# V loaded by casting transfers on the software queue, and channel halves interleaved in V, u and W1

## The chip, the cores and the metric

One core of one Trainium2 chip. The metric is device time in microseconds (us), lower is better. Where two kernels are compared, the ratio is the mean time of one kernel's fast runs over that of the kernel before in the same rounds on the same chip, so not quite the ratio of the medians that are quoted beside it.

## The reference

```python
# u, v: (8, 3008, 256); z: (8, 3008, 64); w_in: (256, 2048); w_out: (2048, 256); all fp32
scores = matmul(z, z.transpose(0, 2, 1)) / 3008
attn   = maximum(scores, 0) ** 2
x      = u * matmul(attn, v)                 # per batch
h      = x.reshape(24064, 256) @ w_in
out    = (h * sigmoid(1.702 * h)) @ w_out
```

## The kernel before

For each of 8 batches the kernel makes the squared scores `a` (matmul "sc", relu on ScalarE, "ACT", square on VectorE, "DVE"), multiplies them with V into `o` (the attention phase, six query chunks), gates `o` with the transposed u into `xt`, and makes the up product `hg` and the down products `st` and `yp`. Scores are symmetric, so about half of the blocks of `a` are not computed but made by DMA transposes (`tt<-a`, `ad<-a`) that the SP engine issues. Transfers that SP issues go by a hardware queue, those that Pool (GpSimd) issues by the software queue. TensorE keeps its order and waits if such a block is late.

V is the stationary operand, in fp16, and 256 channels are two loads of 128 columns (`c` is 0 or 1). In the kernel before, fp32 V comes by the SP queue into a staging tile, and Pool casts it into `V16`, regrouping the channels into two packed halves:

```python
vst = pu.tile([P, VB, D], F32, name="vst", tag="vst", bufs=3)
eng.dma_start(vst[:, :full, :], v[b, ...])                       # SP queue, 512 KB
for k in range(NCC):                                             # 2 casts per 4 key blocks
    pool.tensor_copy(V16[b][:, n0:n0 + VB, k, :].rearrange("p n (q c) -> p n q c", c=QW),
                     vst.rearrange("p n (q k c) -> p n q k c", k=NCC, c=QW)[:, :, :, k, :])
...
# attention: two matmuls on 64 rows each run side by side (upper half of one key block, lower half)
ins = pe.matmul(acc[c][:, :n], V16[b][h, j, c, :], weights(b, i, j)[h], ...)
...
# u comes by Pool's (software) queue; four 128 KB transfers per query chunk, 256-byte runs
eng.dma_start(uq[k * QW:(k + 1) * QW, :n // QW]..., src[:, :, cs])
...
# blocks by symmetry, issued by SP
sp.dma_start_transpose(TT[b, i, cj][:, k0:k0 + 2]..., a...)
...
LOAD = {(3, NJ + 4): 4, (4, NJ + 5): 5}    # (chunk, step of attention): u chunk to load
```

Of the kernel before, what the change touches and what calls it, by code (L numbers as in the profile page):

```python
# [9 lines left out]
F32 = mybir.dt.float32  # L10
F16 = mybir.dt.float16
P = 128
# [3 lines left out]
def kernel(  # L16
# [16 lines left out]
    B, S, D = u.shape  # L33
# [3 lines left out]
    NJ = (S + P - 1) // P  # L37
    S0 = (S // P) * P
    SREM = S - S0
    CH = 512  # L40
# [3 lines left out]
    NCC = D // P  # L44
# [3 lines left out]
    QW = 32  # L48
# [7 lines left out]
    dve, act, pe, sp, pool = nc.vector, nc.scalar, nc.tensor, nc.sync, nc.gpsimd  # L56
# [98 lines left out]

    VB = 4

    def load_v(b, n0, eng):


        if n0 == 0:
            V16[b] = pz.tile([P, NJ, NCC, P], F16, name="V16", tag="V16")
        if b or n0 < 3 * VB:
            vst = pu.tile([P, VB, D], F32, name="vst", tag="vst", bufs=3)
        else:
            vst = pa.tile([P, VB, D], F32, name="vst", tag="tt", bufs=14)
        full = min(VB, NJ - 1 - n0)
        eng.dma_start(vst[:, :full, :], v[b, n0 * P:(n0 + full) * P].rearrange("(n p) c -> p n c", p=P))
        if full < VB:
            for h in range(2):  # L170
                eng.dma_start(vst[h * SREM:(h + 1) * SREM, full, :], v[b, S0:S])
        for k in range(NCC):
            pool.tensor_copy(  # L173
                V16[b][:, n0:n0 + VB, k, :].rearrange("p n (q c) -> p n q c", c=QW),
                vst.rearrange("p n (q k c) -> p n q k c", k=NCC, c=QW)[:, :, :, k, :],
            )

    def width(i):
        return CH if i < NCH - 1 else LAST
# [1 line left out]
    def load_u(b, i):  # L181
        eng = pool if b or i else sp
        n = width(i)
        uq = pu.tile([P, CH // QW, NCC, QW], F32, name="uq", tag="uq")
        src = u[b, i * CH:i * CH + n].rearrange("(q t) c -> t q c", t=QW)
        for k in range(P // QW):
            cs = slice(k * NCC * QW, (k + 1) * NCC * QW)
            eng.dma_start(uq[k * QW:(k + 1) * QW, :n // QW].rearrange("t q k c -> t q (k c)"), src[:, :, cs])  # L188
        UQ[b, i] = uq

    def turn_u(b, i):
        n = width(i)
        ut = pu.tile([P, NCC, CH // QW, QW], F32, name="ut", tag="ut")
        UT[b, i] = ut
        dve.transpose(ut[:, :, :n // QW, :].rearrange("p k q t -> p q k t"), UQ.pop((b, i))[:, :n // QW])



# [84 lines left out]
    def attend(b, i, both=False):  # L283


        n = width(i)
        js, cs = list(range(NJ - 1)), range(2)
        own = i * CB
        if b == 0 and i in (3, 4):
            js = js[own:-CB + 1] + js[:own] + js[-CB + 1:]  # L290
        elif b and i == NCH - 3:
            js = js[own:own + 2] + js[own + CB:-CB + 1] + js[:own] + js[own + 2:own + CB] + js[-CB + 1:]
        elif b and i < NCH - 2:
            js = js[own:own + 2] + js[own + CB:-CB + 1] + js[own + 2:own + CB] + js[:own] + js[-CB + 1:]
        half = [(0, TOP, NJ - 1), (1, LOW, NJ - 1)]
        if both:
            order = [[(c, FULL, j)] for j in js[:-CB] for c in cs] + [[(c, FULL, j)] for c in cs for j in js[-CB:]]
            order.insert(-CB, half)
        elif i == NCH - 1:
            order = [half] + [[(c, FULL, j)] for c in cs for j in js]  # L300
        else:
            order = [[(0, TOP, j), (1, LOW, j)] for j in js] + [half] + [[(1, TOP, j), (0, LOW, j)] for j in js]
        flat = [(k, m) for k, ms in enumerate(order) for m in ms]
        first = {c: next(m for m in flat if m[1][0] == c) for c in cs}
        final = {c: [m for m in flat if m[1][0] == c][-1] for c in cs}
        acc, turn = {}, NJ if order[-1][0][1] != FULL else -1

        def step(k):
            done = []
            for m in order[k]:  # L310
                c, h, j = m
                if (k, m) == first[c]:
                    acc[c] = ps1.tile([P, CH], F32, name="o", tag="ps1")
                ins = pe.matmul(  # L314
                    acc[c][:, :n], V16[b][h, j, c, :], weights(b, i, j)[h],
                    start=(k, m) == first[c], stop=(k, m) == final[c],
                )
                if k == turn:
                    behind(acc["sig"], ins)
                done.append(ins)  # L320
            if k == turn - 1:
                acc["sig"] = post(done)
            for c in cs:
                if k == final[c][0]:
                    gate(c)

        def gate(c):
            ut = UT[b, i][:, c].rearrange("p q t -> p (q t)")
            x = XT[b, i]
            if i < NCH - 1 or b % 2:  # L330
                dve.tensor_tensor(x[:, c, :n], acc[c][:, :n], ut[:, :n], ALU.mult)  # L331
            else:
                dve.tensor_tensor(x[:, c, :LFULL], acc[c][:, :LFULL], ut[:, :LFULL], ALU.mult)
                dve.tensor_tensor(XT[b + 1, i][:, c, LAST:], acc[c][:, LFULL:n], ut[:, LFULL:n], ALU.mult)

        XT[b, i] = XT.get((b, i)) or pa.tile([P, NCC, CH], F16, name="xt", tag="xt", bufs=6)
        if i == NCH - 1 and b % 2 == 0:
            XT[b + 1, i] = pa.tile([P, NCC, CH], F16, name="xo", tag="xo")
        return [lambda k=k: step(k) for k in range(len(order))]


# [43 lines left out]
    def load_w(k):  # L385

        if k == 0:
            hold = const.tile([P, 1], F16, name="hold")
            pool.tensor_copy(hold, XT[0, 1][:, 0, :1])
        if k < 4:  # L390
            w1v = moe_w_in.rearrange("(q k c) f -> q c k f", k=NCC, c=QW)
            pool.dma_start(W1[k * QW:(k + 1) * QW], w1v[k])
        else:
            fs = slice((k - 4) * CB, (k - 3) * CB)
            pool.dma_start(W2[:, fs], moe_w_out.rearrange("(fo p) c -> p fo c", p=P)[:, fs])
# [201 lines left out]
        queue.extend(u_ for i in range(NCH) for u_ in pieces(b, i))  # L597

    fill(0)
    load_v(0, 0, act)  # L600
    first_z((0, CB, 2 * CB, 4 * CB, NJ))
    for n0 in range(VB, NJ, VB):
        load_v(0, n0, sp)
    warm_up(7)
    first_cast(0)
    first_zt(0)
# [11 lines left out]
    for b in range(B):  # L618
        nup = NCH * NFG
        sched, turn, load = (SCHED, TURN, LOAD) if b else (SCHED0, TURN0, LOAD0)  # L620
        head = 0
        for i in range(NCH):
            for n, step in enumerate(attend(b, i, b == 0 and i < 2)):
                if b == 0 and i == 0 and n == 5:
                    load_u(0, 0)
                if b == 0 and i == 0 and n in FIRST_ZT:
                    first_zt(FIRST_ZT[n])
                    if 3 <= FIRST_ZT[n] < NCH - 1:
                        first_cast(FIRST_ZT[n] + 1)
                if (i, n) in turn:  # L630
                    turn_u(b, turn[i, n])
                if (i, n) in load:
                    load_u(b, load[i, n])
                if b == 0 and (i, n) in LOADW:
                    load_w(LOADW[i, n])
                take(b, sched[i].get(n, 0))
                if i == NCH - 1 and n >= HEAD and (n - HEAD) * LAGY // (2 * NJ - 2 - HEAD) >= head and head < LAGY:
                    up_group(b, head)
                    head += 1
                step()  # L640
        more = b + 1 < B
        if more:
            for i in range(2):
                load_u(b + 1, i)
            load_z(b + 1)
            for n0 in range(0, NJ, VB):
                load_v(b + 1, n0, sp)
            fill(b + 1)
        prods = products(nst(b))
        for q in range(head, nup):  # L650
            if more and q in (head + 14, head + 20):
                k = int(q == head + 20)
                turn_u(b + 1, k)
                load_u(b + 1, k + 2)
            up_group(b, q)
            product(b, *prods.pop(0))
        for kp in prods:
            product(b, *kp)
            if SUMS:
                SUMS.pop(0)()  # L660
        if more:
            for k in range(NST, NCH):
                turns, steps = down64(b, k)
                at = {n: 3 - len(turns) for n in turns} | TAIL[len(turns)]
                for n, step in enumerate(steps):
                    take(b + 1, at.get(n, 0))
                    step()
# [30 lines left out]
```

## Time and profile before

| | before |
|---|---|
| median of the first three runs (range) | 1205.64 us (1204.28 to 1205.78) |
| span of the profiled run | 1202.2 us |
| TensorE (PE) busy | 1192.0 us, 99% |
| Pool busy | 308.4 us, of which V casts 91 us |
| PE's waits on DMA transposes | 1.2 us |

PE is TensorE's matmuls, PEld its weight loads. The first part of the page (busy time and instructions of each engine) and its fourth part (the chain of work that ended last, by engine):

```profile
PE 1192.0 (99%) x11785; PEld 723.3 (60%) x11785; DVE 830.6 (69%) x1277; ACT 770.2 (64%) x903; POOL 308.4 (26%) x363
...
PE 97%; DVE 1%; DMA 1%; ACT 0%; issue 0%; ACTq 0%
```

The kernel is bound by TensorE: the chain is nearly all PE. Busy time alone would not show it, since PE is counted busy while matmuls are spread out. Start times of the matmuls do: the columns streamed, at 2.4 GHz and scaled by the share of rows in use, come to about 1157 us (an estimate), and first to last start is 1197 us. (The 2.4 GHz agree with the trace: `hg` matmuls of 512 columns start 216 ns apart and `st` matmuls of 128 columns 56 ns, so 384 columns more take 160 ns, 0.417 ns each.)

Four groups of instructions of the kernel before; the columns are line, engine, operation, output and input, count | busy us and mean ns of one | the engine's idle time just before, and what ended most of it:

```profile
L364 DVE TENSOR_SCALAR gt<-gf 128x1024 f16<-128x1024 f32 (+1 forms) x384 | 275.8, 719 | 89.1 <-ACT gf L363 85.2
L246 DVE TENSOR_TENSOR a<-rl 128x1024 f16<-128x1024 f16 x276 | 192.0, 697 | 183.1 <-ACT rl L232 181.8
L314 PE MATMUL o<-tt,V 64*128 64x512 f16 (+1 forms) x1762 | 215.5, 376 | 1.3 <-DMA tt<-a 1.2
L173 POOL CAST V<-vst 128x512 f16<-128x512 f32 x96 | 91.1, 988 | 61.7 <-DMA vst<-in_v_dram 48.4
```

The same view with shapes kept apart gives the 64-row weight loads of V:

```profile
L314 PEld LDWEIGHTS <-V 64*128 64x128 f16 x3592 | 197.1, 94 | 186.4 <-POOLq L85 4.9 <-DMA tt<-a 2.4 <-issue 1.4
```

A load takes 94 ns in the record, and there are two, for two halves of the rows, in each 216 ns of attention; they overlap, since the 3592 loads add up to 338 us and the busy time is 197.1. The `o<-tt,V` line shows that PE waits for a transposed block only 1.2 us in all. All waits of PE (who waited for whom: us in total, times, longest):

```profile
PE zp L130 <- DVE zst L124: 2.4, 1, 2.4
PE w L97 <- DVE nil L75: 1.2, 1, 1.2
PE o L314 <- DMA tt<-a: 1.2, 2, 0.7
PE sc L218 <- DVE ZT L138: 0.8, 1, 0.8
PE sc L218 <- ACT ZT L136: 0.4, 1, 0.4
```

All but the third belong to the first 16 us. Last, one stretch of batch 0's up phase and one of batch 1's attention (busy us of each engine, granted clock, DMA share, GB/s):

```profile
80.00:150.00 70.00, 69.91 (x647) 45.50 (x645) 62.89 (x100) 50.10 (x61) 29.12 (x30) 1.00 0.51 120
180.00:230.00 50.00, 50.00 (x444) 25.95 (x440) 24.27 (x36) 20.65 (x23) 7.71 (x12) 1.00 0.83 144
```

The columns are stretch, length, then PE, PEld, DVE, ACT, Pool. In attention PE is never idle, and the DMA engines are 83% busy: this is the stage with little room for transfers.

### The profile page before, as it was taken

The numbers are of one execution on the slowest core, as the hardware profiler recorded it, in microseconds if no ns is written. First come the engines' busy times: TensorE is split into PE (matmuls) and PEld (weight loads), VectorE is DVE, ScalarE is ACT, GpSimd is POOL, SyncE is SP. The second block draws the span as 40 slices with busy tenths as digits, with TensorE's granted clock in tenths as the row PEclk, the third lists the DMA queues.
The fourth block names the chain that finished last, engine by engine and source line by source line (L and its number), as shares of the span: only waits on it lengthen the run. The fifth ranks groups of instructions, "written<-read, shape, count | busy, mean of one in ns | idle before, by whom it ended". The sixth has DMA issues, their size and how long they took to land.

```text
span 1202.2 us, 28231 instructions
## 1 busy us (share of the span) xinstructions
PE 1192.0 (99%) x11785; PEld 723.3 (60%) x11785; DVE 830.6 (69%) x1277; ACT 770.2 (64%) x903; POOL 308.4 (26%) x363
## 2 busy tenths in 40 slices
PE   8999999999999999999999999999999999999998
PEld 2445765467654676546765467544775547855577
DVE  6669955597555976469654696638965489564886
ACT  6777684476844768366683666736677366772764
POOL 4144400462003520044200451015520145101000
PEclk9999999999999999999999999999999999999999
DMA  9966379562894639944399454984449854497012
GB/s 214 180 109 125 123 148 169 93 145 82 159 170 90 152 88 167 165 81 137 94 174 156 81 137 102 186 136 77 137 116 173 142 83 141 124 177 126 1 37 71
DMA packets 366592, 152.33 MB, mean 127 GB/s; under 512 B 313312, under 2 KB 358496, under 8 KB 366464
## 3 DMA queue, kind: packets, MB, share of 16 engines
q1 hardware_dynamic: 330320, 114.08, 48.3%
q0 software_dynamic: 35456, 35.86, 14.5%
q8 instruction: 92, 1.51, 0.5%
q10 hardware_dynamic: 688, 0.59, 0.2%
q14 instruction: 36, 0.29, 0.1%
HBM read 60.29 MB, written 24.64 MB: 71 GB/s over the span
## 4 chain that ended last, share of the span: by engine, by line
PE 97%; DVE 1%; DMA 1%; ACT 0%; issue 0%; ACTq 0%
PE o L314 38%; PE hg L355 27%; PE st L455 18%; PE yp L521 8%; PE sc L218 6%; DMA tt<-a 1%; DVE a L246 0%; PE w L97 0%; DVE gt L364 0%; DVE zst L124 0%; ACT gf L363 0%; DVE s L428 0%; PE zp L130 0%; ACT rl L232 0%; DVE s L426 0%
## 5 line engine op out<-in xcount | busy, mean ns | idle before, releaser
L363 ACT ACTIVATE gf<-hg 128x1024 f32<-128x1024 f32 (+1 forms) x384 | 385.7, 1007 | 164.4 <-PE hg L355 136.9
L232 ACT ACTIVATE rl<-sc 128x1024 f16<-128x1024 f32 x311 | 308.1, 1025 | 208.0 <-PE sc L218 206.0
L314 PEld LDWEIGHTS <-V 64*128 64x128 f16 (+1 forms) x4052 | 241.2, 94 | 243.4 <-issue 10.2
L355 PE MATMUL hg<-xt,W 128*128 128x512 f16 (+1 forms) x1408 | 354.5, 374 | 0.1
L364 DVE TENSOR_SCALAR gt<-gf 128x1024 f16<-128x1024 f32 (+1 forms) x384 | 275.8, 719 | 89.1 <-ACT gf L363 85.2
L246 DVE TENSOR_TENSOR a<-rl 128x1024 f16<-128x1024 f16 x276 | 192.0, 697 | 183.1 <-ACT rl L232 181.8
L314 PE MATMUL o<-a,V 64*128 64x512 f16 (+2 forms) x2010 | 318.3, 373 | 0.0
L188 POOL DMA_DIRECT2D uq<-in_u_dram x188 | 129.5, 696 | 512.6 <-PE sc L218 342.1
L314 PE MATMUL o<-tt,V 64*128 64x512 f16 (+1 forms) x1762 | 215.5, 376 | 1.3 <-DMA tt<-a 1.2
L355 PEld LDWEIGHTS <-W 128*128 128x128 f16 x1536 | 141.2, 98 | 117.4 <-issue 0.3
L455 PEld LDWEIGHTS <-gt 128*128 128x128 f16 x2176 | 132.4, 98 | 28.7
L218 PE MATMUL sc<-ZT 64*128 64x512 f16 (+1 forms) x692 | 122.3, 367 | 1.6 <-DVE ZT L138 0.8
L455 PEld LDWEIGHTS <-s 128*128 128x128 f16 x1632 | 99.2, 98 | 20.7
L173 POOL CAST V<-vst 128x512 f16<-128x512 f32 x96 | 91.1, 988 | 61.7 <-DMA vst<-in_v_dram 48.4
L521 PE MATMUL yp<-W,gt 64*128 64x256 f16 x1664 | 103.9, 269 | 0.0
L521 PEld LDWEIGHTS <-gt 64*128 64x128 f16 x1664 | 80.4, 94 | 19.2 <-POOLq L85 4.1
L331 DVE TENSOR_TENSOR xt<-o,ut 128x512 f16<-128x512 f32 x80 | 51.5, 685 | 38.1 <-PE o L314 38.1
L455 PE MATMUL st<-WT,gt 128*128 128x128 f16 x1088 | 71.8, 219 | 0.0
L455 PE MATMUL st<-W,gt 128*128 128x128 f16 x1088 | 71.7, 219 | 0.0
L455 PE MATMUL st<-WT,s 128*128 128x128 f16 x1088 | 71.5, 219 | 0.0
L465 ACT ACTIVATE uP<-st 128x256 f32<-128x256 f32 x102 | 39.1, 383 | 38.7 <-DVE y L471 33.7
L218 PEld LDWEIGHTS <-ZT 64*128 64x128 f16 x692 | 38.2, 94 | 37.6 <-issue 7.3
(47 smaller groups left out, 629.3 us busy)
## 6 DMA issues: line engine op xcount, KB each, us to landing
vst<-in_v_dram SPq DMA_DIRECT2D x39, 512.0 KB, 4.9
uq<-in_u_dram POOLq DMA_DIRECT2D x156, 128.0 KB, 3.5
out_dram<-y SPq DMA_DIRECT2D x33, 512.0 KB, 3.9
tt<-a SPq DMA_TRANSPOSE x230, 3.4
uq<-in_u_dram POOLq DMA_DIRECT2D x32, 112.0 KB, 2.9
out_dram<-y POOLq DMA_DIRECT2D x7, 512.0 KB, 4.9
vst<-in_v_dram SPq DMA_DIRECT2D x8, 384.0 KB, 4.6
out_dram<-y POOLq DMA_DIRECT2D x7, 384.0 KB, 3.2
```

The source lines that it names most:

```text
L173: pool.tensor_copy(V16[b][:, n0:n0 + VB, k, :].rearrange("p n (q c) -> p n q c", c=QW), vst.rearrange("p n (q k c) -> p n q k c", k=NCC, c ...
L188: eng.dma_start(uq[k * QW:(k + 1) * QW, :n // QW].rearrange("t q k c -> t q (k c)"), src[:, :, cs])
L218: pe.matmul(sc[:, r, :m * P], zt[h, 2 * kp + r, :], zt[h, (qi + 1) * CB - m:(qi + 1) * CB, :], start=True, stop=True,)
L232: act.activation(rl, sc, AF.Relu, scale=csc)
L246: dve.tensor_tensor(a, rl, rl, ALU.mult)
L314: ins = pe.matmul(acc[c][:, :n], V16[b][h, j, c, :], weights(b, i, j)[h], start=(k, m) == first[c], stop=(k, m) == final[c],)
L331: dve.tensor_tensor(x[:, c, :n], acc[c][:, :n], ut[:, :n], ALU.mult)
L355: pe.matmul(hg[:, e, :n], W1[:, c, ff * P:(ff + 1) * P], XT[b, i][:, c, :n], start=(c == 0), stop=(c == NCC - 1),)
L363: act.activation(gf[:, :, :n], hg[:, :, :n], AF.Gelu_apprx_sigmoid, scale=1.0 / FSC)
L364: dve.tensor_scalar(g, gf[:, :, :n], FSC, None, ALU.mult)
L455: pe.matmul(bank[:, m, :], lhs()[:, f, m, :], right[:, ff, :], start=name in ("P1", "P2", "P5") and m == 0 and ff == 0, stop=ff == NFF // ...
L521: ins = pe.matmul(yp[s // per][:, s % per, :], GT[b, k, ff // CB][h, ff % CB, s * P:(s + 1) * P], W2[h, ff, :], start=new, stop=n == last[ ...
```

## The change

If partition p holds channels 2p and 2p + 1, then V can stay in its natural order in `V16`, and half `c` is every second column. Then no regrouping is needed, and a transfer can cast V and put it straight into place. A transfer that casts has to be issued from Pool: the Trainium skill, "DMA: Bandwidth & Descriptors", Rules for kernel authors, says so. u and W1 take the same order of channels. The intent is to free Pool, and VectorE beside it, of 84 of 96 casts, and SP of 56 transfers. The diff, cut:

```diff
-    def load_v(b, n0, eng):
+    def load_v(b, n0):
-            V16[b] = pz.tile([P, NJ, NCC, P], F16, ...)
+            V16[b] = pz.tile([P, NJ, D], F16, ...)
+        if b:
+            dst, eng = V16[b][:, n0:n0 + VB], pool          # cast by the transfer, into place
+        elif n0 < 3 * VB:
+            dst, eng = pu.tile([P, VB, D], F32, ... tag="vst", bufs=3), sp if n0 else act
...
-        for k in range(NCC):
-            pool.tensor_copy(V16[b][:, n0:n0 + VB, k, :]..., vst...[:, :, :, k, :])
+        if b == 0:
+            for n in range(0, VB, 2):
+                pool.tensor_copy(V16[b][:, n0 + n:n0 + n + 2], dst[:, n:n + 2])
...
-        uq = pu.tile([P, CH // QW, NCC, QW], F32, ...)
+        uq = pu.tile([P, CH // QW, QW, NCC], F32, ...)       # turned by reading every second fp32
...
-                    acc[c][:, :n], V16[b][h, j, c, :], weights(b, i, j)[h],
+                    acc[c][:, :n], V16[b][h, j].rearrange("p (c k) -> p k c", k=NCC)[:, c], weights(b, i, j)[h],
...
-            w1v = moe_w_in.rearrange("(q k c) f -> q c k f", k=NCC, c=QW)
+            w1v = moe_w_in.rearrange("(q c k) f -> q c k f", k=NCC, c=QW)
```

More of the change, by code (lines that the diff above doesn't have):

```diff
@@ L156 @@
     VB = 4
-    def load_v(b, n0, eng):
+    def load_v(b, n0):
         if n0 == 0:
-            V16[b] = pz.tile([P, NJ, NCC, P], F16, name="V16", tag="V16")
-        if b or n0 < 3 * VB:
-            vst = pu.tile([P, VB, D], F32, name="vst", tag="vst", bufs=3)
+            V16[b] = pz.tile([P, NJ, D], F16, name="V16", tag="V16")
+        if b:
+            dst, eng = V16[b][:, n0:n0 + VB], pool
+        elif n0 < 3 * VB:
+            dst, eng = pu.tile([P, VB, D], F32, name="vst", tag="vst", bufs=3), sp if n0 else act
         else:
-            vst = pa.tile([P, VB, D], F32, name="vst", tag="tt", bufs=14)
+            dst, eng = pa.tile([P, VB, D], F32, name="vst", tag="tt", bufs=14), sp
         full = min(VB, NJ - 1 - n0)
-        eng.dma_start(vst[:, :full, :], v[b, n0 * P:(n0 + full) * P].rearrange("(n p) c -> p n c", p=P))
+        eng.dma_start(dst[:, :full, :], v[b, n0 * P:(n0 + full) * P].rearrange("(n p) c -> p n c", p=P))
         if full < VB:
             for h in range(2):
-                eng.dma_start(vst[h * SREM:(h + 1) * SREM, full, :], v[b, S0:S])
-        for k in range(NCC):
-            pool.tensor_copy(
-                V16[b][:, n0:n0 + VB, k, :].rearrange("p n (q c) -> p n q c", c=QW),
-                vst.rearrange("p n (q k c) -> p n q k c", k=NCC, c=QW)[:, :, :, k, :],
-            )
+                eng.dma_start(dst[h * SREM:(h + 1) * SREM, full, :], v[b, S0:S])
+        if b == 0:
+            for n in range(0, VB, 2):
+                pool.tensor_copy(V16[b][:, n0 + n:n0 + n + 2], dst[:, n:n + 2])
     def width(i):
@@ L183, in load_u @@
         n = width(i)
-        uq = pu.tile([P, CH // QW, NCC, QW], F32, name="uq", tag="uq")
+        uq = pu.tile([P, CH // QW, QW, NCC], F32, name="uq", tag="uq")
         src = u[b, i * CH:i * CH + n].rearrange("(q t) c -> t q c", t=QW)
@@ L187, in load_u @@
             cs = slice(k * NCC * QW, (k + 1) * NCC * QW)
-            eng.dma_start(uq[k * QW:(k + 1) * QW, :n // QW].rearrange("t q k c -> t q (k c)"), src[:, :, cs])
+            eng.dma_start(uq[k * QW:(k + 1) * QW, :n // QW].rearrange("t q c k -> t q (c k)"), src[:, :, cs])
         UQ[b, i] = uq
@@ L194, in turn_u @@
         UT[b, i] = ut
-        dve.transpose(ut[:, :, :n // QW, :].rearrange("p k q t -> p q k t"), UQ.pop((b, i))[:, :n // QW])
+        dve.transpose(
+            ut[:, :, :n // QW, :].rearrange("p k q t -> p q k t"),
+            UQ.pop((b, i))[:, :n // QW].rearrange("p q c k -> p q k c"),
+        )
     def folded(b, i):
@@ L599 @@
     fill(0)
-    load_v(0, 0, act)
+    load_v(0, 0)
     first_z((0, CB, 2 * CB, 4 * CB, NJ))
     for n0 in range(VB, NJ, VB):
-        load_v(0, n0, sp)
+        load_v(0, n0)
     warm_up(7)
@@ L646 @@
             for n0 in range(0, NJ, VB):
-                load_v(b + 1, n0, sp)
+                load_v(b + 1, n0)
             fill(b + 1)
```

## The prediction

> **What bounds the kernel now.** TensorE. The profile's first part has PE busy 1192.0 of 1202.2 us; the chain that ended last is 97% PE (attention product "o" 38%, "hg" 27%, "st" 18%). Busy alone proves little, so I took matmul starts from the trace: columns / 2.4 GHz, scaled by rows / 128, sum to about 1157 us (an estimate) against 1197 us from first to last start. The 40 us between are mostly a fixed 2 to 2.5 ns per matmul (10 us in "st") and about 10 us of start-up. In the waits view PE waited about 6 us in all, and nothing in batches 1 to 7 waited for V; in batch 0 PEld waited 0.3 us for it.
>
> **What the change moves.**
> 1. Pool: 84 of 96 V casts go (0.99 us mean, 83 us). 56 casting V transfers come. The load of W2 has the same 128x4x256 shape and casts too: 0.77 us issue, 6.1 us to landing. 42 x 0.77 + 14 x 0.6 = about 40 us. Pool falls from 308 to about 265 us. Batch b+1's V is issued 20 to 35 us after attention of batch b ends and is needed over 60 us later. All off the critical path.
> 2. VectorE: in the first 15 us a two-input square takes 1.09 us beside a Pool cast, 0.69 us without. Fewer casts shorten VectorE's sums in the up phase (0.71 to 0.79 us mean), perhaps 5 to 10 us of 830; PE was not waiting for them. Batch 0 keeps 12 casts, now contiguous, each delivering both channel halves of two key blocks: one early PE pause (0.6 us at 10 us) may shrink, but VectorE's squares at 12 to 15 us probably absorb it: gain 0 to 0.5 us.
> 3. VectorE's transpose of u reads every second fp32: 48 x 1.21 us now. I expect 1.2 us still: the Trainium skill, "SBUF — State Buffer", box on cachelines, gives 16-byte lines and wants two hits per line; stride 8 bytes has two. No run yet shows it. If it doubled: +58 us VectorE, mostly hidden.
> 4. TensorE: all 4512 weight loads of V read with a step of 2 elements. This alone is on the critical path. The record shows a load as 4 chunks of 32 columns, 94 ns. In attention a pair of half-row matmuls starts every 216 ns, each load 1 to 2 ns after its half's previous matmul, so it has about 120 ns of slack. The skill's "TensorE: Matmul & The Clock Gate", section on Fast Weight Load, says the chunks may be packed or strided, so the fast form should stay. I expect 94 to 120 ns, hidden. Matmul count and order do not change.
>
> **Predicted time.** 1204.5 us (before 1205.64); 8 in 10 between 1201 and 1208.5. Faster by over 2%: 1%. Within 2%: 96%. Slower by over 2%: 3%.
>
> **What would show it.** Pool busy near 265 us, casts x12; V on the software queue; V weight loads 94 to 120 ns and pairs still 216 ns apart; transposes still 1.2 us; PE busy 1190 to 1195 us; no PE wait on a V transfer.
>
> **What would make it wrong.** A strided load that loses the fast form: two loads per 216 ns no longer hide; pairs at 230 ns or more would add 25 us or more over about 390 us of pairs. Or a slower u transpose in the up phase, where VectorE is busy 90%, holding back gelu scaling and so PE. Or V transfers starved of descriptors while VectorE is busy, landing after attention starts.

## The result, and the profile after

| | before | changed |
|---|---|---|
| median of four runs (range) | 1205.42 us (1204.28 to 1205.78) | 1207.68 us (1204.96 to 1210.22) |
| ratio, 95% interval | | 1.002, 0.9996 to 1.0044 |
| Pool busy | 308.4 us | 281.5 us |
| VectorE busy | 830.6 us | 811.2 us |
| PE's waits on DMA transposes | 1.2 us, 2 waits | 6.6 us, 5 waits |

The changed kernel is correct, within 2% of the one before, and if anything slower. Five more runs below (e1) make it 1.003, with an interval that excludes 1. The first and fourth part of its page:

```profile
PE 1192.3 (99%) x11785; PEld 720.4 (60%) x11785; DVE 811.2 (67%) x1277; ACT 773.3 (64%) x903; POOL 281.5 (23%) x335
...
PE 95%; DMA 3%; DVE 1%; ACT 1%; issue 0%; SPq 0%; ACTq 0%
```

Groups of the changed kernel, then its 64-row weight loads of V, with the columns as before:

```profile
L177 POOL CAST V<-vst 128x512 f16<-128x512 f32 x12 | 8.8, 775 | 7.0 <-DMA vst<-in_v_dram 6.8
L171 POOL DMA_DIRECT2D V<-in_v_dram x42 | 37.5, 902 | 0.0
L174 POOL DMA_DIRECT2D V<-in_v_dram x14 | 7.9, 570 | 0.0
L368 DVE TENSOR_SCALAR gt<-gf 128x1024 f16<-128x1024 f32 (+1 forms) x384 | 266.9, 695 | 108.3 <-ACT gf L367 100.8
L318 PE MATMUL o<-tt,V 64*128 64x512 f16 (+1 forms) x1762 | 215.3, 376 | 6.7 <-DMA tt<-a 6.6
L196 DVE STREAM_TRANSPOSE ut<-uq 128x1024 f32<-128x1024 f32 (+1 forms) x48 | 58.3, 1216 | 0.0
```

```profile
L318 PEld LDWEIGHTS <-V 64*128 64x128 f16 x3592 | 194.5, 94 | 195.2 <-issue 6.2 <-DMA tt<-a 6.0 <-POOLq L85 5.3
```

Pool has 12 casts of V left, and 56 issues of V transfers in place of the other 84. A strided weight load takes the same 94 ns. The transpose of u, which now reads every second element, takes 1.22 us as it did (1.21). And the DMA share of the chain went from 1% to 3%, with PE waiting 6.6 us for transposed blocks. PE's waits on them, then the same two stretches as before:

```profile
PE o L318 <- DMA tt<-a: 6.6, 5, 1.8
```

```profile
80.00:150.00 70.00, 70.00 (x647) 45.62 (x646) 60.02 (x100) 50.58 (x61) 24.73 (x26) 1.00 0.55 97
180.00:230.00 50.00, 48.22 (x434) 22.57 (x429) 23.18 (x34) 18.98 (x21) 7.71 (x12) 1.00 0.89 144
```

In the up phase VectorE and Pool are both lighter, as intended, and PE takes no notice: it was full there before. In attention, where V is not moving at all, PE lost 1.8 of 50 us.

To see where time goes, I took from each trace, for each batch, the time from the first to the last attention matmul (`o`) start. In every profiled run here the stretches between attention phases are 62.6 to 62.8 and 65.9 to 66.0 us by turns and the last one 61.8 us, so all that differs lies in attention (and, for batch 0, in the start). Its floor is 83.1 us. One profiled run each, batches 1 to 7, in us:

| run | 1 | 2 | 3 | 4 | 5 | 6 | 7 | sum over 7 x 83.1 |
|---|---|---|---|---|---|---|---|---|
| before | 83.1 | 83.1 | 83.1 | 83.7 | 84.0 | 83.3 | 83.1 | 1.7 |
| changed | 85.2 | 83.1 | 84.9 | 83.4 | 85.1 | 84.3 | 83.5 | 7.8 |

Where the text below gives a wait of PE inside a batch, it is the distance of two matmul starts less the usual 216 ns; the profile's own figure, as in the lines shown, is about 0.18 us less.

**Batch 1 closely.** Pool's instructions around 42 us into batch 1's attention (start us, duration, engine, line, what, count, [idle before <- releaser]), first in the kernel before:

```profile
209.14 2.61 POOL L188 DMA_DIRECT2D uq<-in_u_dram  x4 [39.19 <-PE sc L218]
```

and in the changed kernel:

```profile
209.27 0.69 POOL L189 DMA_DIRECT2D uq<-in_u_dram  x1 [39.33 <-PE sc L222]
210.43 1.94 POOL L189 DMA_DIRECT2D uq<-in_u_dram  x3 [0.47 <-issue]
```

and SP's there, before and changed:

```profile
210.81 3.67 SPq L253 DMA_TRANSPOSE tt<-a  x2
```

```profile
210.95 3.91 SPq L257 DMA_TRANSPOSE tt<-a  x2
```

The four loads of a u chunk are issued while SP issues two transposes that PE needs soon. In the changed kernel Pool pauses 0.47 us after the first load, for nothing that the profile shows ("issue"). What PE does a little later in the changed kernel:

```profile
217.76 0.59 PE L318 MATMUL o<-ad,V 64*128 64x512 f16 x4
220.14 1.04 PE L318 MATMUL o<-tt,V 64*128 64x512 f16 x8 [1.78 <-DMA tt<-a]
```

and in the kernel before:

```profile
217.61 0.61 PE L314 MATMUL o<-ad,V 64*128 64x512 f16 x4
218.04 1.04 PE L314 MATMUL o<-tt,V 64*128 64x512 f16 x8
```

By the landings in the trace (us from the start of that attention phase), the last u load landed at 49.4 before and at 52.1 changed; the two transposes, issued at 43.5 and 45.6 us before and 0.1 us later in the changed kernel, landed at 49.4 and 50.0 before, at 51.9 and 52.8 changed, and PE stood still. This looks as if the u load and the transposes delay one another; e9 tests it.

### The profile page after: what moved, and what is told of

It is laid out like the page before. It is cut to its first block, busy times and chain, and to the rows that moved or that the text cites. A ratio compares the mean times of both kernels' runs of the same rounds, so it can differ in the third digit from the quotient of the medians.

```text
span 1208.4 us, 28111 instructions
## 1 busy us (share of the span) xinstructions
PE 1192.3 (99%) x11785; PEld 720.4 (60%) x11785; DVE 811.2 (67%) x1277; ACT 773.3 (64%) x903; POOL 281.5 (23%) x335
## 4 chain that ended last, share of the span: by engine, by line
PE 95%; DMA 3%; DVE 1%; ACT 1%; issue 0%; SPq 0%; ACTq 0%
PE o L318 37%; PE hg L359 27%; PE st L459 18%; PE yp L525 7%; PE sc L222 6%; DMA tt<-a 3%; DVE a L250 1%; ACT rl L236 1%; DMA zf<-in_z_dram 0%; DVE zst L124 0%; PE zp L130 0%; DVE ZT L138 0%; SPq L257 0%; ACT y L538 0%; DVE y L475 0%
## 5 line engine op out<-in xcount | busy, mean ns | idle before, releaser
L318 PEld LDWEIGHTS <-V 64*128 64x128 f16 (+1 forms) x4052 | 238.7, 95 | 252.8 <-issue 15.5
L368 DVE TENSOR_SCALAR gt<-gf 128x1024 f16<-128x1024 f32 (+1 forms) x384 | 266.9, 695 | 108.3 <-ACT gf L367 100.8
L335 DVE TENSOR_TENSOR xt<-o,ut 128x512 f16<-128x512 f32 x80 | 51.5, 685 | 38.1 <-PE o L318 38.1
L153 POOL COPY zst<-zst 128x768 f16<-128x768 f16 x14 | 53.5, 3823 | 55.0 <-DMA zst<-in_z_dram 55.0
L196 DVE STREAM_TRANSPOSE ut<-uq 128x1024 f32<-128x1024 f32 (+1 forms) x48 | 58.3, 1216 | 0.0
```

Source lines behind the costliest of these rows:

```text
L153: pool.tensor_copy(zst[:, :, 1, :], zst[:, :, 0, :])
L196: dve.transpose(ut[:, :, :n // QW, :].rearrange("p k q t -> p q k t"), UQ.pop((b, i))[:, :n // QW].rearrange("p q c k -> p q k c"),)
L318: ins = pe.matmul(acc[c][:, :n], V16[b][h, j].rearrange("p (c k) -> p k c", k=NCC)[:, c], weights(b, i, j)[h], start=(k, m) == first[c], s ...
L368: dve.tensor_scalar(g, gf[:, :, :n], FSC, None, ALU.mult)
```

## The experiments

The first four ran on one chip, e5 to e8 on another, e9 to e11 on a third. Theories: S, strided weight reads slow the transposes; D, V's transfers on the software queue do; N, chance.

### e1: the changed kernel again

No edit.

> The changed kernel unaltered, to learn its spread: it had 1204.96 to 1210.22 us in four runs against 1204.28 to 1205.78 of the kernel before, and its profiled run lost 6.6 us of PE to five waits on the DMA transposes of a (1.2 us in two waits before). Theory N (nothing systematic; the late transposes are chance): ratio to before 1.000 to 1.001, interval holding 1. Theory S (the strided weight reads make the transposes' DMA later): ratio about 1.002. Theory D (the V transfers moved to the software queue do it): ratio about 1.002.

Measured: 1209.01 us median (1207.01 to 1209.42), before 1204.37; ratio 1.003, interval 1.0018 to 1.0042. N falls: the change costs about 0.3%. The clock does not explain it: the runs at a mean clock of 0.998 took 1207.66, 1209.01 and 1209.18 us here and 1203.22 to 1206.72 us in the kernel before. Batch 1 shows the same pause (Pool's record at the same place):

```profile
209.16 0.69 POOL L189 DMA_DIRECT2D uq<-in_u_dram  x1 [39.19 <-PE sc L222]
210.31 1.94 POOL L189 DMA_DIRECT2D uq<-in_u_dram  x3 [0.47 <-issue]
```

### e2: packed weights (wrong result)

```diff
-  V16[b][h, j].rearrange("p (c k) -> p k c", k=NCC)[:, c]
+  V16[b][h, j, c * P:(c + 1) * P]
```

> Wrong result on purpose: as the changed kernel, but the weight loads of V read 128 packed columns (c*128 onward) in place of every second one; everything else, the V transfers too, is unaltered. My prediction holds strided loads to be free: weight loads 94 ns, pairs 216 ns apart and time equal to e1 within 0.1 to 0.2%. Theory S: back at 1205.4 us with a small spread, below e1 by about 2 us. Theory D: as e1. Theory N: as e1 and as before.

Measured: 1209.22 us (1206.78 to 1213.36), ratio 1.0038 (1.0023 to 1.0054). The result was wrong, as it had to be. With packed loads the loss stays, so S falls. The median load is 94 ns and pairs are 216 ns apart in before, e1 and e2 alike. In batch 1 the longest wait of this trace (2.35 us at 53.1 us) was followed at once by 3.41 us at half clock, with pairs 420 ns apart, so that the batch lost 4.0 us and not 2.4.

### e3: interleaved, but cast on Pool

```diff
-        if b:
-            dst, eng = V16[b][:, n0:n0 + VB], pool
-        elif n0 < 3 * VB:
+        if b or n0 < 3 * VB:
             dst, eng = <staging tile>, sp if b or n0 else act
...
-        if b == 0:
-            for n in range(0, VB, 2): pool.tensor_copy(...)
+        for n in range(0, VB, 2): pool.tensor_copy(...)
```

> Half the change: channels interleaved and weight loads strided as in the changed kernel, but V of every batch still comes as fp32 by the SP queue and is cast on Pool (96 packed casts), as in the kernel before. Theory D: back at 1205.4 us. Theory S: about 2 us above before, as e1. Theory N: all alike. Pool busy back at about 310 us and VectorE's sums in the up phase back at 0.74 to 0.79 us mean, with no effect on PE.

Measured: 1204.62 us (1203.35 to 1205.68), ratio 0.9997 (0.9984 to 1.001). Correct. The interleaving alone costs nothing that these runs show; the loss lies in V's way in. Pool was busy 306 us again and VectorE's sums took 0.72 to 0.79 us, as expected. PE's wait on transposes in e3:

```profile
PE o L315 <- DMA tt<-a: 1.8, 4, 0.6
```

### e4: weight loads with a step of 16 (wrong result)

```diff
-  V16[b][h, j].rearrange("p (c k) -> p k c", k=NCC)[:, c]
+  V16[b].rearrange("p n d -> p (n d)")[h, (j % 12) * D + c:(j % 12) * D + c + 16 * P - 15:16]
```

> Wrong result on purpose: the weight loads of V read with a step of 16 elements (32 bytes, every element in a line of its own) in place of 2. If a load is free because two elements still share a 16-byte line (cacheline theory), loads now take longer than 94 ns in the record, up to about double, and if that exceeds about 120 ns more, pairs stand over 216 ns apart and the kernel gains tens of us. If the fast load does not mind steps at all, loads stay 94 ns and time stays within 0.3% of e1. Up to 5 us may be added at the start, where batch 0's first weights now wait for later V blocks.

Measured: 1209.98 us (1208.91 to 1215.06), ratio 1.0051 (1.0032 to 1.0069). The 64-row loads of e4:

```profile
L318 PEld LDWEIGHTS <-V 64*128 64x128 f16 x3592 | 272.7, 142 | 128.4 <-DMA tt<-a 10.1 <-POOLq L85 5.4 <-issue 2.0
```

A load takes 142 ns, half again as long, and still fits: pairs stay 216 ns apart, and batch 2's attention takes the floor of 83.1 us. (Two loads of 142 ns are more than 216 ns, but they overlap: 3592 of them are 510 us, and the busy time is 272.7.) The first attention matmul starts at 12.1 us in place of 8.5, as foreseen for the later V blocks. The profiled run, the slowest of the four, also lost 4.9 us in batch 6, to a wait of 3.1 us followed by 3.41 us at half clock. So two readings of the step are told apart: it is not true that the load minds no step, but step 2 costs nothing (where between 2 and 16 the cost begins was not run), and even the 48 ns more of step 16 hid in the slack of about 120 ns.

### e5: Pool's casts, and the casting transfers besides

As e3, with V's casting transfers also issued on the software queue, into the same V, in the same place of Pool's order; the casts then overwrite it.

```diff
+            for n0 in range(0, NJ, VB):
+                pool.dma_start(V16[b + 1][:, n0:n0 + VB][:, :full, :], <same rows of v>)   # and the two remainders
             for n0 in range(0, NJ, VB):
                 load_v(b + 1, n0)       # SP transfer and Pool casts, as in e3
```

> As e3 (V by the SP queue, cast on Pool), and in addition the 56 casting V transfers of the changed kernel on the software queue, in the same place of Pool's order, written to the same V and then overwritten by the casts: the software queue's sequence of transfers is that of the changed kernel, the SP queue's that of the kernel before. Theory P (the sequence on the software queue fixes where a pause of about 0.5 us falls between u loads, and where it falls in batches 1 and 6 the u load and two DMA transposes of a land 2 to 3 us late): pauses after the first u load of the group at 42 us into attention in batches 1 and 6, PE waits of 0.7 to 3 us at 51 to 54 us there, ratio about 1.003. Theory Q (it is V's absence from the SP queue that does it): no such waits, ratio about 1.000. Pool and DMA are busier in the up phase, where PE should not notice.

Measured: 1208.24 us (1202.94 to 1210.44), before 1203.73; ratio 1.0033 (1.0016 to 1.0049). The pauses are where the changed kernel has them (0.47 us in batch 1, 0.50 in batch 6), with PE waits of 1.55 us at 52.3 and 0.80 us at 51.5 us. So Q falls: SP's queue has its V loads back, and the loss is there. What costs is 56 transfers more on the software queue, long landed by then.

### e6: the sequence shifted by four transfers

```diff
+        if k == 7:     # once, after the last W2 load of batch 0
+            extra = pu.tile([P, CH // QW, NCC * QW], F32, name="extra", tag="vst", bufs=3)
+            for g in range(4): pool.dma_start(extra[g * QW:(g + 1) * QW], <a u chunk, as load_u reads it>)
```

> The changed kernel plus four spare u loads [...] into a free buffer, once, in batch 0 while Pool is idle. Theory P: the pauses move four transfers earlier, to idle places (in batch 1 from the second u load of the group to a u load of the up phase), so batches 1 and 6 lose their waits at 51 to 54 us; other batches may gain one; ratio to before 1.000 to 1.002. Theory Q, or any theory that needs no sequence: the waits stay in batches 1 and 6, ratio 1.003.

Measured: 1204.79 us (1203.87 to 1204.98), ratio 1.0008 (0.9996 to 1.002). More work brought the ratio down by 0.2% (e5 and e7, on the same chip, have 1.0033; the interval of e7 does not reach below 1.0021), so the sequence on the software queue does matter. Part of the 0.2% is clock (mean 0.9996 here, 0.9986 in e7), but the runs at 0.999 alone stay apart: 1204.79 and 1204.98 us here, 1206.11 to 1209.11 in e7. In detail theory P holds only in part: batch 6 lost its pause and its wait, batch 4 gained a pause (0.50 us) and a wait of 0.82 us, but batch 1 lost its pause and kept a wait of 1.49 us. Its u loads were issued as in the kernel before (41.8 to 43.8 us) and still landed at 51.5. The pause is therefore one way to the late landing and not the only one.

### e7: a move that moved nothing

```diff
-    LOAD = {(3, NJ + 4): 4, (4, NJ + 5): 5}
+    LOAD = {(4, 2): 4, (4, NJ + 5): 5}
```

> The changed kernel, but the u load that is issued 42 us into attention (query chunk 4) is issued about 4.6 us later, after the two transposes of a that it collided with (43.5 and 45.6 us) have been issued. If the collision is what costs, those two land by about 49 us in all batches, the waits at 51 to 54 us go in every batch, pause or not, and the ratio falls from 1.003 to about 1.001; the waits at 6 to 7 us in odd batches stay. If the u load then lands too late for its turning, a new wait appears at 56 us.

Measured: 1207.16 us (1206.11 to 1209.11), ratio 1.0033 (1.0021 to 1.0045). The u load was still issued at 41.8 to 43.8 us in most batches. The order of instructions on Pool was the same, and Pool, which had nothing else to wait for, ran the load as early as before. This is a failed experiment on the theory, and in effect a third sample of the changed kernel: 1.002, 1.003, 1.0033.

### e8: as e7, and the last stores on ACT's queue

```diff
-                store(b, k, pool)
+                store(b, k, act)
```

> As e7, and the stores of the last two output chunks of a batch are issued by ACT on its own hardware queue in place of Pool. They overlap six transposes at the start of the next attention, where odd batches (3, 5, 7) of the changed kernel lose 1 to 2 us at 6 to 7 us. If the software queue's share is what delays these transposes, they land 1 to 2 us sooner and the waits go: about 83.1 us of attention in each of batches 1 to 7 and a ratio of 0.998 to 0.999. If any transfer of that size there does it, the waits stay and the ratio is as e7.

Measured: 1206.13 us (1203.46 to 1206.74), ratio 1.0013 (1.0001 to 1.0026). Better than e7, and short of what was expected: waits at 6 to 7 us shrank to one of 0.43 us, but new ones of 0.24 us for scores appeared at 3.2 us in odd batches, two of about 0.6 us at 51 to 52 us stayed, and there were two of 0.5 to 0.7 us elsewhere (batches 5 and 7). As two things changed (the engine of the store, and 14 transfers fewer in the software sequence), it settles nothing by itself.

### e9: the u load held back

```diff
-    LOAD = {(3, NJ + 4): 4, (4, NJ + 5): 5}
+    LOAD = {(4, NJ + 5): 5}
...
+                if b and (i, n) == (4, 0):
+                    post(done)          # Pool waits for these matmuls
+                    load_u(b, 4)
```

> What e7 meant to do and did not (its u load was still issued at 42 us, since moving it in the program did not move it past anything that Pool waits for). Here Pool waits for the first matmuls of query chunk 4, so the changed kernel's u load for that chunk is issued at about 47 us into attention, after the two transposes that were issued at 43.5 and 45.6 us. If the collision costs, these transposes land by about 49 us in each of batches 1 to 7, the waits at 51 to 54 us vanish in the trace (0.7 to 3 us in batches 1 and 6 until now) and the ratio falls from 1.003 to 1.000 to 1.001; waits at 6 to 7 us in odd batches stay. If it does not, the waits stay where they were.

Measured: 1204.95 us (1202.38 to 1206.41), before 1204.39; ratio 0.9998 (0.9984 to 1.0012). Correct. Pool's record in batch 1 of e9:

```profile
214.57 0.69 POOL L189 DMA_DIRECT2D uq<-in_u_dram  x1 [44.79 <-PE o L318]
215.73 1.94 POOL L189 DMA_DIRECT2D uq<-in_u_dram  x3 [0.47 <-issue]
```

The pause is still there, but it harms nothing: the two transposes landed at 47.8 and 49.0 us, and at 50.7 us at the latest in any batch, and no batch has a wait at 51 to 54 us. With the load held back (e9 to e11) the first of the two takes 3.0 to 4.4 us to land in all 21 batches traced; beside the load it takes 4.6 to 9.1 us in all 70. So it is the collision of this u load with these transposes that cost; the pause by itself does not. What remained in the trace were two long waits of 1.99 us (1.81 in the profile's figure) at 7.3 us in batches 5 and 7:

```profile
PE o L318 <- DMA tt<-a: 3.8, 3, 1.8
```

### e10: and the last stores put off

```diff
-                store(b, k, pool)
+                LATER.append(lambda: store(b, k, pool))
...
+                if (i, n) == (NCH - 1, 2):     # query chunk 5 of the next attention
+                    while LATER: LATER.pop(0)()
```

> As e9, and the two stores of the last output chunks that Pool issues at -5 and 2 us of the next batch's attention, beside six transposes, are put off to query chunk 5 (about 58 us), where the queues are idle. If software-queue traffic beside transposes is what costs, all waits on transposes at 6 to 7 us vanish too, attention takes 83.1 to 83.5 us in each of batches 1 to 7, and the ratio is 0.998 to 0.999: faster than both kernels by 1 to 2 us. If transposes are late for another reason, waits at 6 to 7 us stay and the ratio is as e9.

Measured: 1203.86 us (1203.61 to 1204.93), ratio 0.9996 (0.9984 to 1.0009). Correct. All waits at 6 to 7 us are gone; each attention phase takes 83.1 to 83.5 us. PE's wait on transposes in e10:

```profile
PE o L318 <- DMA tt<-a: 0.6, 2, 0.3
```

The two waits left are at about 30 us, where other kernels here, the one before among them, have some too; they were not studied. The changed kernel thus lost its 0.3% and is level with the kernel before; the interval does not show it faster, and the 0.998 to 0.999 that I expected was too much.

### e11: both moves in the kernel before

> The kernel before, with both moves of e10. If V's path matters only through these collisions, it comes out equal to e10 within 0.1%, at 0.998 to 0.999. If V on the software queue costs in some other way too, e10 stays 0.1 to 0.3% above this one.

Measured: 1203.21 us (1202.02 to 1203.97), ratio 0.9988 (0.9976 to 1.0001). Equal to e10 within the intervals. It is the fastest median of all, 0.1% ahead of the kernel before, though its interval still touches 1. Two of its five runs had a clock of 1.000; at 0.998 it took 1203.21 to 1203.97 us and e10 1203.61 and 1203.86. This is the fair comparison, since the moves may help the kernel before too: V's new path costs 0.3% without them and 0.08%, within the noise, with them.

The attention phases of the profiled runs, as in the table above:

| run | 1 | 2 | 3 | 4 | 5 | 6 | 7 | sum over 7 x 83.1 | ratio |
|---|---|---|---|---|---|---|---|---|---|
| e1 changed again | 85.2 | 83.1 | 83.1 | 83.1 | 84.2 | 83.8 | 84.4 | 5.2 | 1.003 |
| e2 packed weights | 87.1 | 83.2 | 83.1 | 83.1 | 84.5 | 84.1 | 83.4 | 6.8 | 1.0038 |
| e3 casts on Pool | 83.6 | 83.1 | 83.1 | 84.4 | 83.4 | 83.8 | 83.1 | 2.8 | 0.9997 |
| e4 step 16 | 84.2 | 83.1 | 83.3 | 83.6 | 84.8 | 88.0 | 84.8 | 10.1 | 1.0051 |
| e5 both | 84.6 | 83.1 | 83.9 | 83.1 | 83.1 | 83.9 | 83.6 | 3.6 | 1.0033 |
| e6 shifted | 84.6 | 83.5 | 83.2 | 84.1 | 84.1 | 83.3 | 83.1 | 4.2 | 1.0008 |
| e7 not moved | 85.1 | 83.1 | 83.4 | 83.1 | 85.1 | 84.2 | 83.7 | 6.0 | 1.0033 |
| e8 stores by ACT | 84.1 | 83.5 | 83.9 | 83.1 | 84.4 | 83.1 | 83.8 | 4.2 | 1.0013 |
| e9 held | 83.1 | 83.1 | 83.1 | 83.1 | 85.1 | 83.4 | 85.1 | 4.3 | 0.9998 |
| e10 held, deferred | 83.5 | 83.1 | 83.1 | 83.1 | 83.5 | 83.1 | 83.3 | 1.0 | 0.9996 |
| e11 in before | 83.1 | 83.1 | 83.1 | 83.1 | 84.2 | 83.1 | 83.6 | 1.6 | 0.9988 |

A row is one run out of four to six, so it names places and does not size them; the ratios do. (Batch 0's attention took 94.6 or 94.7 us in e6, e7 and e11 and 96.1 in before. The clock goes with this difference: e6 and e11 have no half-clock stretch near it and e7's came earlier, at 7.8 us, while the trace of before has one of 3.41 us at 16.8 us.)

## Why the prediction was right, and where it was not

- **The verdict and the range held.** 1207.68 us lies in 1201 to 1208.5, and the change is within 2%. It was near the upper end, though: I put the change at 1.1 us faster, and it is 2 to 4 us slower. The median of e1, 1209.01 us, would have lain just outside. The verdict held because every term is small beside 2%. That the number fell in the range was in part luck: the change that I named had the wrong sign, and the cost that appeared was not among my terms.
- **TensorE bounds it, strided loads hide: right.** Loads 94 ns (I allowed 94 to 120), pairs 216 ns, and e2 shows the time unmoved by packing. The Trainium skill's "TensorE: Matmul & The Clock Gate", Weight-path perf modes, says that the chunks of a fast weight load may be packed or strided; the trace agrees. A slip: there are 4052 such loads in the trace, not 4512; the group that I added was already counted in.
- **Cachelines: in agreement, and now with a number.** "SBUF — State Buffer", in its box on cachelines, gives 16-byte lines and asks for two hits per line. A step of 4 bytes cost nothing in a weight load and 8 bytes nothing in the transpose of u (1.22 us); a step of 32 bytes took a load from 94 to 142 ns.
- **Pool and VectorE: right in kind, off in size.** Pool fell by 27 us and not 43: the casting issues took 46 us and not 40, and the copies of z (`zst`), which now run at other moments beside VectorE, took 53.5 us in place of 42.2. VectorE fell by 19 us, not 5 to 10: the sums that took 0.71 to 0.79 us took 0.68 to 0.74, and 0.72 to 0.79 again with the casts back (e3). Two engines that get in each other's way is what "SBUF — State Buffer", section on the two sides, describes as a shared port pair; the trace agrees in direction. PE was not waiting for either, as said.
- **The step that failed is item 1's last sentence, "All off the critical path".** I checked only that V itself would land in time. It does: no wait of PE names a V transfer. (Even its times were off: V was issued 3 to 10 us after attention ended, not 20 to 35, and had landed by 19 us, over 40 us before the next attention.) The term was put at 0 and measures about 0.3%, some 4 us. Through the sequence of the software queue, V's transfers change when later u loads are issued, or land, and those share the DMA engines with transposes that PE needs at once, in a stage that is 83% full. "DMA: Bandwidth & Descriptors", Issuing engines are not separate DMA queues, says that all queues run on the same 16 DMA engines and interleave; the trace agrees, and I had read the kernel as if separate queues kept these apart.

What is shown: the loss goes with the casting V transfers on the software queue (e1, e3, e5), not with strided reads (e2) nor with the SP queue's emptier sequence (e5); it is paid where the u load meets two transposes (gone in e9) and where the last stores meet six (gone in e10). The last two were measured against the kernel before on a third chip, where the changed kernel without the moves was not run again, and where the waits went is read from one trace of each. What stays open: why Pool pauses about 0.5 us between u loads at places that the software sequence fixes, and by what means the sequence delays the landing of a load that has no pause (batch 1 of e6) or the stores of odd batches. The names of theories P and Q in the expectations are of these two questions: Q fell, P holds for the sequence, but its pause is not the whole cause.

## What to carry to other kernels

A transfer that lands long before it is needed can still cost, by shifting the transfers behind it on its queue into those that the bounding engine needs at once; so ask of a moved transfer what it displaces, not only whether it is in time. Look for the stage where the DMA engines are nearly full, and put loads and stores with slack outside it, behind a wait that the issuing engine really has: moving a line in the program moves nothing if its engine was idle. A wait of the bounding engine can also cost more than itself: after the two longest inside attention, of 2.4 and 3.1 us, the clock was at half for 3.41 us. A strided stationary operand was free here at a step of 2 and hidden at 16, so a layout can be chosen for the transfers.

## What the Trainium skill lacked or had wrong

- "TensorE: Matmul & The Clock Gate", Weight-path perf modes: it says which steps are allowed, not what they cost. Here a 64-row, 128-column fp16 load took 94 ns packed, 94 ns at a step of 2 and 142 ns at a step of 16, with pairs of matmuls 216 ns apart in all three.
- "DMA: Bandwidth & Descriptors": nothing on pauses between transfers of the software queue. Here Pool paused 0.32 to 0.53 us between two u loads, at the same places in every profiled run of the changed sequence of transfers and at others when four transfers were added.
- The same page says that transfers of all queues interleave, but gives no figure for a DMA transpose beside other loads. Here the transpose issued at 43.5 us took 3.0 us to land in most batches when the u load was held back, and 4.6 to 9.1 us beside it in all runs.
- The same page's rule to issue casting transfers from GpSimd gives no figure for what such an issue costs Pool. Here one of 128x4x256 took 0.74 to 1.21 us of Pool and landed after 7.9 us (median), beside a busy VectorE.
